# Row maxima in single PSUM banks of one ring of six, part of v's split on GpSimd, and a written-out order for the first two pairs of heads

## The chip, the cores and the metric

The kernel runs on one core of one Trainium2 chip. The metric is device time in microseconds (us), the median of repeated runs. A core has five instruction queues that matter here: TensorE (PE, matmuls; PEld is its weight load), VectorE (DVE), ScalarE (ACT), GpSimd (POOL) and SyncE (SP, which only issues DMAs). Each runs its instructions in order and stops at the first one whose inputs, or whose output buffer, aren't ready.

## What is computed

Attention in which a query sees only the keys of its own cluster, and behind it a mixture of experts on the attention's output:

```python
def _attn_ref(q, k, v, centroids):
    ...
    q_assign = np.argmax(np.einsum('bhsd,hcd->bhsc', q_n, c_n), axis=-1)
    k_assign = np.argmax(np.einsum('bhsd,hcd->bhsc', k_n, c_n), axis=-1)
    mask = q_assign[:, :, :, None] == k_assign[:, :, None, :]
    scores = scale * np.matmul(q, k.transpose(0, 1, 3, 2))
    scores = np.where(mask, scores, -1000000000.0)
    scores = scores - np.max(scores, axis=-1, keepdims=True)
    attn = np.exp(scores)
    ...
    return np.matmul(attn, v)
```

Four batches, eight heads, 768 tokens, 64 columns a head, 16 clusters. The experts (8 of them, the best two for each of the 3072 tokens) take 512 columns to 1024 and back.

## The kernel before

The heads go in 16 pairs (four batches of four pairs); a pair is `p`, its two heads `s`. Float32 numbers are split into an upper and a lower half, so that TensorE can work with shorter types and lose little. For each pair:

- `load_qk` brings q and k, `a_hi` (ACT) and `a_lo` (DVE, some on POOL) split them. From pair 2 on `a_hi` writes a copy into a PSUM bank and `a_lo` subtracts from it. `b_place` copies the halves by DMA into the two big operand tiles A and Bt (three sets, used in turn).
- `a_sims`, `a_copy`, `a_turn`, `a_max1`, `a_ge`, `a_ky`, `a_max2`, `a_eq`, `a_mask` find the clusters; `b_mask` adds them to A by DMA, so that one matmul gives a score with the mask in it.
- `b_max` (line 541): for each head and each of six blocks of 128 queries, two matmuls of 128x384 (L546) give all 768 scores of upper halves; one DVE reduction over 768 columns (L549) takes their maximum. The two matmuls write a tile `wide` of two PSUM banks, of which there is one.
- `b_neg` and `b_negT` turn the 12 maxima of a pair into two rows of Bt.
- `scores` (L577): per step four matmuls and two exponentials (ACT, L578); `split_p` (L589, POOL) takes the lower half of 768 exponentials; `values` (L610 to L616) multiplies with v, four steps later.

v comes in half batches of four heads: `load_v`, `v_max` (DVE, L386), `v_scale` (a matmul, L397, and two small DVE operations) and, head by head, `v_split` (L411): ACT scales v into a PSUM bank (L415), ACT takes the upper half of it (L416), DVE subtracts for the lower half (L417).

PSUM has eight banks. In the attention one is `aux` (maxima and small sums), one `av` (the values), two are `wide`, and four are a `ring` that everything else takes its banks from (`ps()`). In the experts `wide`'s two banks are given to the ring as `ring2`.

The order of the work is written by hand. `attention` fills a table `sched`: `at(step, f, ...)` puts a part at a step, with steps of 12 to a pair; numbers for it stand in `AT` (lines 28 to 40). Each step then issues its table entries around `scores`, `split_p` and `values` of a step four back. Everything at step -24 comes first, before the first scores (step 0); the first pair's parts stand there (`f0`), head by head, the second pair has numbers of its own (`p1`, steps -21 to -13, and its masks at 0.333). An order in the table is the order in every engine's queue. A ring bank is handed out when its part is issued, and the first instruction that writes it waits until the last reader of the tile that had the bank is done.

Of the kernel before, what the change touches and what calls it, by code (L numbers as in the profile page):

```python
# [9 lines left out]
F32 = mybir.dt.float32  # L10
# [26 lines left out]
    thr=5.0, bmax0=[-20.333, -1.333], bstep0=[1.0, 0.667], neg0=[-15.0, 2.667], negT0=[-14.667, 3.333],  # L37
    p1=dict(hstep=0, hi=[-21.0, -21.0], lo=[-13.667, -13.667], place=-13.0, sims=-18.333, copy=-18.333, turn=-16.333, max1=-14.333,
            ge=-14.333, max2=-14.333, eq=-14.333, ky=-14.333, mask=0.333, bmask=0.333),
# [7 lines left out]
class Kernel:  # L47
    def __init__(self, ctx, tc, qk, v, cent, w_gate, w_noise, noise, w1, w2, out):
# [16 lines left out]
        self.more_banks, self.turns = None, 0  # L65
# [131 lines left out]
    def attention(self, ctx):  # L197
        nc, tc = self.nc, self.tc
        B, H, S, D, NJ = self.B, self.H, self.S, self.D, self.NJ
        self.psum2 = ctx.enter_context(tc.tile_pool(name="psum2", bufs=1, space=PSUM))  # L200
# [25 lines left out]
        for p in range(NP):  # L226
            b, hp = divmod(p, H // 2)
            w = 12 * (p - 2)
            if hp == 0:
                for g in range(2):  # L230
                    v = w + 24 * g
                    V = T["fv"][g] if p == 0 else T
                    at(22.333 if (b, g) == (1, 0) else v + V["v"], self.load_v, b, g)
# [17 lines left out]
            if p == 0:  # L251
                f0 = lambda f, *a: at(-24, f, *a)
                f0(self.load_qk, 0, 0)
                f0(self.load_qk, 0, 1)
                f0(self.load_qk, 1)
                for s in range(2):
                    for i in range(2):
                        f0(self.a_hi, p, i, s)
                    if s == 0:
                        f0(self.c_turn)  # L260
                        f0(self.fixed_init, 0)
                        f0(self.constants2)
                    for i in range(2):
                        f0(self.a_lo, p, i, s)
                f0(self.fixed_init, 1)
                f0(self.fixed_init, 2)
                f0(self.b_place, p, 0, 0)
                for s in range(2):
                    for f in (self.a_sims, self.a_copy, self.a_turn, self.a_max1, self.a_ge, self.a_ky, self.a_max2,
                              self.a_eq, self.a_mask, self.b_mask):  # L270
                        f0(f, p, s)
                    f0(self.b_place, p, 1, s)
                    if s == 0:
                        f0(self.b_place, p, 0, 1)
# [1137 lines left out]
```

## Time and profile before

| | us |
|---|---|
| median of 3 runs | 1099.83 (1098.12 to 1108.2) |
| the profiled execution | 1095.88 |
| its span, first to last instruction | 1094.0 |
| TensorE busy | 968.3 (89%) |
| VectorE busy | 662.2 (61%) |
| GpSimd busy | 549.9 (50%) |
| ScalarE busy | 493.0 (45%) |

The span has two parts: the attention, to about 518 us, and the experts behind it. The shares are means over both. A matmul's busy time holds its pipeline, so TensorE that reads as busy is not at its peak. The granted TensorE clock is a share of 2.4 GHz: 1.00 is 2.4, 0.50 is 1.2.

### The profile page before, as it was taken

Reading aid. Unit: us, or ns where it says so; the run is one execution under the profiler, and the core shown is the slowest. Engines: PE = TensorE matmul, PEld = TensorE weight load, DVE = VectorE, ACT = ScalarE, POOL = GpSimd, SP = SyncE. Lnnn points to the kernel's source line nnn. Section 1 sums busy time; section 2 is a strip of 40 time slices with the busy share of each in tenths; the row PEclk is TensorE's granted clock in tenths of the full one; section 3 lists DMA queues with packets and bytes.
Section 4 is the critical chain, followed back from the end, with each engine's and each line's share of the span. In section 5 each row is a group of like instructions: output and inputs, shape, how many; then the busy total and the mean of one; then the engine's idle time right before and its main releaser. Section 6 shows DMA issues by size and latency. Waiting matters only on the chain.

```text
span 1094.0 us, 21139 instructions
## 1 busy us (share of the span) xinstructions
PE 968.3 (89%) x8020; PEld 615.8 (56%) x8020; DVE 662.2 (61%) x1254; ACT 493.0 (45%) x1100; POOL 549.9 (50%) x609
## 2 busy tenths in 40 slices
PE   4378788888888888879999999999999999999994
PEld 1256667666677667668455545545455454554542
DVE  4456677787777877778655654555445564454511
ACT  3245665665667575647713522415224152241510
POOL 9135566666996679777244524325242252433211
PEclk9868999999999999999999999999999999999998
DMA  5636487776878787633639772946829266293200
GB/s 157 175 88 168 117 195 188 165 190 150 192 168 181 158 182 170 139 120 86 175 105 212 172 204 81 209 133 161 199 86 239 95 168 194 74 202 122 63 33 33
DMA packets 164252, 162.74 MB, mean 149 GB/s; under 512 B 87945, under 2 KB 140041, under 8 KB 164146
## 3 DMA queue, kind: packets, MB, share of 16 engines
q1 hardware_dynamic: 150476, 124.65, 48.6%
q0 software_dynamic: 13296, 36.38, 11.7%
q8 instruction: 64, 1.05, 0.4%
q10 hardware_dynamic: 374, 0.32, 0.1%
q14 instruction: 42, 0.34, 0.1%
HBM read 78.21 MB, written 26.51 MB: 96 GB/s over the span
## 4 chain that ended last, share of the span: by engine, by line
PE 44%; issue 5%; POOL 1%; ACT 0%; DVE 0%; DMA 0%; POOLq 0%; ACTq 0%
PE ring L1301 22%; PE ring L1339 20%; PE ring L1329 1%; POOL out L1351 1%; POOL xt L1314 1%; PE ring L1332 1%; PE ring L1206 0%; PE ring L721 0%; PE ring L886 0%; DMA out<-yo,idx 0%; PE ring L729 0%; PE ring L1197 0%; ACT gxT L723 0%; ACT w2t L1185 0%; DVE pl L589 0%
## 5 line engine op out<-in xcount | busy, mean ns | idle before, releaser
L589 POOL TENSOR_TENSOR pl<-pe 128x768 f16<-128x768 f32 x173 | 253.5, 1472 | 144.7 <-ACT pe L578 93.5
L1301 PE MATMUL ring<-xT,w1t 128*128 128x416 f16 (+2 forms) x1536 | 272.8, 339 | 0.1
L1339 PE MATMUL ring<-w2t,hT 128*128 128x512 f16 x1152 | 252.5, 379 | 0.6 <-ACT w2t L1185 0.5
L578 ACT ACTIVATE pe<-ring 128x384 f32<-128x384 f32 x384 | 168.2, 489 | 171.0 <-PE ring L577 165.2
L549 DVE TENSOR_REDUCE aux<-wide 128x1 f32<-128x768 f32 x192 | 185.0, 964 | 89.3 <-PE wide L546 86.5
L1301 PEld LDWEIGHTS <-w1t 128*128 128x128 f16 x1536 | 149.3, 98 | 118.8 <-issue 0.8
L546 PE MATMUL wide<-A 128*128 128x384 f32 x384 | 126.7, 409 | 71.1 <-DVE aux L549 60.0
L1178 ACT ACTIVATE hr<-ring 128x416 f32<-128x416 f32 (+2 forms) x128 | 66.5, 519 | 270.7 <-PE ring L1301 268.3
L1339 PEld LDWEIGHTS <-hT 128*128 128x128 f16 x1152 | 112.2, 98 | 134.1 <-issue 1.5
L1351 POOL DMA_INDIRECT out<-yo,idx x52 | 62.4, 1199 | 226.9 <-DVE yo L1347 109.8
L577 PE MATMUL ring<-A 128*128 128x384 f32 x384 | 138.2, 360 | 3.6 <-ACT pe L578 1.9
L577 PE MATMUL ring<-B 128*128 128x384 f32 x384 | 132.7, 346 | 0.0
L1181 DVE TENSOR_TENSOR hT<-hr,hT 128x416 f16<-128x416 f32 (+3 forms) x128 | 71.2, 559 | 83.8 <-ACT hT L1180 83.5
L546 PEld LDWEIGHTS wide<-A 128*128 128x128 f32 x384 | 62.8, 203 | 96.9 <-DVE aux L549 81.7
L1347 DVE SCALAR_TENSOR_TENSOR yo<-ring,we,xt 128x512 f32<-128x512 f32 (+1 forms) x49 | 36.7, 748 | 122.8 <-PE ring L1339 107.5
L610 PE MATMUL av<-vv,pe 128*128 128x65 f16 x1152 | 98.9, 196 | 0.1
L612 PE MATMUL av<-vv,pe 128*128 128x64 f16 x1152 | 97.6, 193 | 0.0
L1281 POOL DMA_INDIRECT xg<-xs,idx x52 | 56.4, 1085 | 81.6 <-DMA xT<-xg 71.3
L610 PEld LDWEIGHTS <-pe 128*128 128x128 bf16 x1152 | 78.4, 99 | 27.0 <-issue 25.4
L612 PEld LDWEIGHTS <-pe 128*128 128x128 bf16 x1152 | 79.2, 99 | 0.2
L577 PEld LDWEIGHTS ring<-A 128*128 128x128 f32 x384 | 74.5, 194 | 8.4 <-ACT pe L578 3.7
L577 PEld LDWEIGHTS ring<-B 128*128 128x128 f32 x384 | 74.7, 194 | 0.0
(218 smaller groups left out, 1177.3 us busy)
## 6 DMA issues: line engine op xcount, KB each, us to landing
stg<-in_moe_w SPq DMA_DIRECT2D x64, 512.0 KB
qt<-in_qk SPq DMA_DIRECT2D x15, 768.0 KB
A<-hl SPq DMA_DIRECT2D x28, 384.0 KB
B<-hl SPq DMA_DIRECT2D x28, 384.0 KB
B<-hl SPq DMA_DIRECT2D x32, 192.0 KB
vt<-in_v SPq DMA_DIRECT2D x8, 768.0 KB
out<-zt SPq DMA_DIRECT2D x12, 512.0 KB
xs<-xh SPq DMA_DIRECT2D x15, 384.0 KB
```

The source lines that it names most:

```text
L546: nc.tensor.matmul(t[:, n], A[:, 0, s, j * 128:j * 128 + 128], A[:, 1, s, n * 384:n * 384 + 384], start=True, stop=True)
L549: nc.vector.tensor_reduce(self.aux[:, c:c + 1], t, axis=XY, op=OP.max, negate=True)
L577: nc.tensor.matmul(t, M[:, 1 - qi, s, ks], M[:, qi, s, ns], start=not qi, stop=bool(qi))
L578: nc.scalar.activation(pe[:, n], t, AF.Exp, scale=self.scale)
L589: (nc.vector if last else nc.gpsimd).tensor_tensor(lo, pe, hi, op=OP.subtract)
L610: nc.tensor.matmul(av[:, j, :], ph[:, js], vv[:, hh, kj, 64:129], start=(kc == 0 and j == 0), stop=False, skip_group_check=True)
L612: nc.tensor.matmul(av[:, j, :64], ph[:, js], vv[:, hh, kj, 0:64], start=False, stop=False, skip_group_check=True)
L1178: nc.scalar.activation(r[:, :n], p, AF.Relu, scale=2.0 ** -HT)
L1181: nc.vector.tensor_tensor(h1, r[:, a:b], h0, op=OP.subtract)
L1301: nc.tensor.matmul(p, self.w1t[:, wi, c, f * 128:f * 128 + 128], self.xT[e][:, c, xi, n0:n1], start=(i == 0), stop=(i == 3 * ND - 1))
L1339: nc.tensor.matmul(p, self.hT[:, hi, f, t * 128:t * 128 + 128], self.w2t[:, wi, f], start=(i == 0), stop=(i == 3 * NF - 1))
L1351: i = nc.gpsimd.indirect_dma_start(out=self.out, out_offset=bass.IndirectOffsetOnAxis(ap=en[:r], axis=0), in_=yo[:r], in_offset=None, boun ...
```

## The change

Four things are done.

1. The ring has six banks from the start, `wide` and `ring2` are gone. `b_max` takes two single banks of the ring, and each gets a reduction of its own over 384 columns: the first into `aux` as before, the second into a small SBUF tile `mm`. `b_neg` has one more operation, the minimum of both (the maxima are negated).
2. `v_split` scales v in place in SBUF, and GpSimd subtracts.
3. The first pair's parts, the second pair's up to its masks, and the first `load_v` are issued in one written-out order (`first`). The numbers `p1`, `bmax0[0]`, `neg0[0]`, `negT0[0]` are gone.
4. The lower halves of the first pair's second head go from POOL to DVE, those of the second pair from DVE to POOL. Four placements of the first pair (`b_place(0, 1, 0, dma)`) are issued by ACT's queue.

```diff
     def ps(self):
-        self.turns += 1
-        if self.more_banks and self.turns % 3 == 0:
-            return self.more_banks.tile([128, 512], F32, name="ring2", bufs=2)
-        return self.psum.tile([128, 512], F32, name="ring", bufs=4)
+        return self.psum.tile([128, 512], F32, name="ring", bufs=6)
...
-                f0(self.load_qk, 0, 0)
...
+    def first(self, do):
+        dma = self.nc.scalar
+        do(self.load_qk, 0, 0)
+        do(self.load_qk, 0, 1)
+        do(self.load_qk, 1)
...
+        do(self.b_place, 0, 1, 0, dma)
+        do(self.a_copy, 1)
+        do(self.b_place, 0, 1, 1)
+        do(self.load_v, 0, 0)
+        for j in range(self.NJ):
+            do(self.b_max, 0, 0, j)
+            if j == 1:
+                do(self.a_turn, 1)
+        for i in range(2):
+            do(self.b_place, 1, i)
+        do(self.b_neg, 0, 0, 1)
+        do(self.b_negT, 0, 0, 1)
+        for f in (self.a_max1, self.a_ge, self.a_ky, self.a_max2, self.a_eq, self.a_mask, self.b_mask):
+            do(f, 1)
...
     def v_split(self, b, g, h):
         nc, D = self.nc, self.D
         vv, am = self.vv[b, g], self.am[b, g]
-        t = self.ps()[:, :384].rearrange("p (j d) -> p j d", d=D)
-        nc.scalar.activation(t, self.vt[b, g][:, h], AF.Copy, scale=am[:, 2:3])
+        t = self.vt[b, g][:, h]
+        nc.scalar.activation(t, t, AF.Copy, scale=am[:, 2:3])
         nc.scalar.activation(vv[:, h, :, 64:128], t, AF.Copy)
-        nc.vector.tensor_tensor(vv[:, h, :, 0:64], t, vv[:, h, :, 64:128], op=OP.subtract)
+        nc.gpsimd.tensor_tensor(vv[:, h, :, 0:64], t, vv[:, h, :, 64:128], op=OP.subtract)
...
-            (self.nc.gpsimd if s else self.nc.vector).tensor_tensor(hl[:, 3 - 3 * i, a:b], qt[:, i, a:b], hl[:, 1 + i, a:b],
+            (self.nc.gpsimd if p else self.nc.vector).tensor_tensor(hl[:, 3 - 3 * i, a:b], qt[:, i, a:b], hl[:, 1 + i, a:b],
...
     def b_max(self, p, s, j):
 
         nc, st, A = self.nc, self.st[p], self.A[p % 3]
+        if (s, j) == (0, 0):
+            st["mm"] = self.wk.tile([128, 2 * self.NJ], F32, name="mm")
         c = self.NJ * s + j
-        t = self.psum2.tile([128, 2, 512], F32, name="wide", bufs=1)[:, :, :384]
         for n in range(2):
-            nc.tensor.matmul(t[:, n], A[:, 0, s, j * 128:j * 128 + 128],
+            t = self.ps()[:, :384]
+            nc.tensor.matmul(t, A[:, 0, s, j * 128:j * 128 + 128],
                              A[:, 1, s, n * 384:n * 384 + 384], start=True, stop=True)
-        c += 488 + 12 * (p % 2)
-        nc.vector.tensor_reduce(self.aux[:, c:c + 1], t, axis=XY, op=OP.max, negate=True)
+            m = 488 + 12 * (p % 2) + c
+            o = st["mm"][:, c:c + 1] if n else self.aux[:, m:m + 1]
+            nc.vector.tensor_reduce(o, t, axis=X, op=OP.max, negate=True)
 
     def b_neg(self, p, s, n):
 
-        v, W, c = self.nc.vector, n * self.NJ, 488 + 12 * (p % 2) + self.NJ * s
-        o = self.aux[:, c:c + W]
+        v, W, c = self.nc.vector, n * self.NJ, self.NJ * s
+        m = 488 + 12 * (p % 2) + c
+        o = self.aux[:, m:m + W]
         hi, lo = (self.nm[:, W * i:W * i + W] for i in range(2))
+        v.tensor_tensor(o, o, self.st[p]["mm"][:, c:c + W], op=OP.min)
```

What this does to SP's queue at the start, before the first scores. `A_115` and `B_118` (after: `A_112` and `B_115`) are the second pair's A and Bt, `qt` is a load of q and k (the first in these rows belongs to the third pair, the second to the fourth), `vt` the first load of v. Before:

```order
L373 DMA qt<-in_qk 128x1536
L516 DMA A_115<-xt 64x4x384
L516 DMA A_115<-xt 32x2x384 x2
...
L516 DMA B_118<-xt 32x4x384
L380 DMA vt<-in_v 128x1536
L373 DMA qt<-in_qk 128x1536
L516 DMA A_115<-mk 16x2x384 x2
```

After:

```order
L403 DMA vt<-in_v 128x1536
L539 DMA A_112<-xt 64x4x384
L539 DMA A_112<-xt 32x2x384 x2
...
L539 DMA B_115<-xt 32x4x384
L539 DMA A_112<-mk 16x2x384 x2
L396 DMA qt<-in_qk 128x1536 x2
```

The load of v went ahead of the second pair's ten placements; the load of the third pair's q and k went from ahead of them to behind them and behind the mask's two.

What it does to DVE's queue in the middle of the attention, where a half batch of v is split. Line 549 (after: 575) is the maximum, 439 (462) the lower halves of q and k, 417 the lower half of v. Before:

```order
L549 TENSOR_REDUCE aux<-wide 128x1
L439 TENSOR_TENSOR hl<-ring,hl 128x384
L417 TENSOR_TENSOR vv<-ring,vv 128x6x64
L549 TENSOR_REDUCE aux<-wide 128x1
L417 TENSOR_TENSOR vv<-ring,vv 128x6x64
L549 TENSOR_REDUCE aux<-wide 128x1
```

After:

```order
L575 TENSOR_REDUCE aux<-ring 128x1
L575 TENSOR_REDUCE mm<-ring 128x1
L462 TENSOR_TENSOR hl<-ring,hl 128x384
L575 TENSOR_REDUCE aux<-ring 128x1
L575 TENSOR_REDUCE mm<-ring 128x1
```

Each maximum has become two rows, and the subtractions of v that stood between the maxima are gone from this queue.

Those subtractions stand in POOL's queue now, between the lower halves of the exponentials (line 617, before 589), which followed each other there before. After:

```order
L617 TENSOR_TENSOR pl<-pe 128x768
L440 TENSOR_TENSOR vv<-vt,vv 128x6x64
L617 TENSOR_TENSOR pl<-pe 128x768
L440 TENSOR_TENSOR vv<-vt,vv 128x6x64
L617 TENSOR_TENSOR pl<-pe 128x768 x2
L709 TENSOR_TENSOR xh<-xp,xh 128x6x64
```

Each is an operation of 128 partitions by 384 elements on the queue that had none of them.

## Rows read from the trace of the kernel before

**Rows 1.** Busy us by stage: PE, PEld, DVE, ACT, POOL; clock, DMA share, GB/s.
```profile
40.00:130.00 90.00, 63.07 (x579) 47.98 (x577) 51.65 (x91) 45.18 (x101) 37.03 (x30) 0.83 0.52 128
130.00:477.50 347.50, 291.01 (x3798) 241.86 (x3796) 259.31 (x537) 219.61 (x515) 256.52 (x226) 1.00 0.77 176
518.30:1094.00 575.70, 559.62 (x3001) 284.15 (x2996) 294.72 (x514) 192.08 (x411) 197.85 (x278) 0.99 0.55 141
```

**Rows 2.** Waits from 130 to 477.5: us in total, times, longest.
```profile
DVE aux L549 <- PE wide L546: 58.3, 81, 2.1
PEld wide L546 <- DVE aux L549: 45.8, 44, 2.0
PE wide L546 <- DVE aux L549: 35.2, 41, 1.7
...
DVE vv L417 <- ACT vv L416: 18.9, 22, 1.4
```

**Rows 3.** PE's waits from 40 to 130: the same columns.
```profile
PE wide L546 <- DVE aux L549: 13.0, 16, 1.9
PE ring L397 <- DVE vm L386: 9.2, 1, 9.2
```

**Rows 4.** Timeline at 60: start, us, engine, line, idle before and what ended it.
```profile
59.97 0.16 DVE L558 SCALAR_TENSOR_TENSOR nm<-aux,nm 128x6 fp32r<-128x6 f32 x1
...
61.26 0.62 PE L546 MATMUL wide<-A 128*128 128x384 f32 x2 [0.60 <-DVE aux L549]
...
61.92 0.97 DVE L549 TENSOR_REDUCE aux<-wide 128x1 f32<-128x768 f32 x1 [0.26 <-PE wide L546]
62.94 0.62 PE L546 MATMUL wide<-A 128*128 128x384 f32 x2 [1.06 <-DVE aux L549]
```

**Rows 5.** Groups by line: count, busy us, mean ns of one, idle before.
```profile
L589 POOL TENSOR_TENSOR pl<-pe 128x768 f16<-128x768 f32 x173 | 253.5, 1472 | 144.7 <-ACT pe L578 93.5 <-PE av L616 32.6 <-ACT nt L565 10.7
...
L681 POOL TENSOR_TENSOR xh<-xp,xh 128x384 f16<-128x384 f32 x26 | 24.0, 924 | 16.7 <-ACT xh L677 16.7
...
L417 DVE TENSOR_TENSOR vv<-ring,vv 128x384 f16<-128x384 f32 x32 | 17.8, 557 | 26.8 <-ACT vv L416 26.8
```

**Rows 6.** Three DVE reductions by line: ns shortest/median/longest, first and last start, forms.
```profile
L549 DVE TENSOR_REDUCE aux<-wide x192: 954/967/967, 18.6 to 494.3; 128x1 f32<-128x768 f32 x192
...
L475 DVE TENSOR_REDUCE mx<-ring x17: 358/547/549, 9.1 to 452.1; 128x24 f32<-128x384 f32 x15, 128x12 f32<-128x192 f32 x2
...
L386 DVE TENSOR_REDUCE vm<-vt x8: 1743/1745/1756, 50.7 to 416.0; 128x1 bf16<-128x1536 f32 x8
```

**Rows 7.** Timeline of the start (SPq is SP issuing DMAs).
```profile
11.06 1.95 POOL L441 TENSOR_TENSOR hl<-qt,hl 128x384 fp32r<-128x384 f32 x2
...
16.56 4.10 SPq L516 DMA_DIRECT2D A<-hl  x6
...
20.23 0.73 POOL L363 MEMSET B<- 2x768 f32 x1
...
25.32 0.53 SPq L373 DMA_DIRECT2D qt<-in_qk  x1
...
40.04 1.13 ACT L578 ACTIVATE pe<-ring 128x384 f32<-128x384 f32 x2 [4.89 <-PE ring L577]
...
46.29 0.33 SPq L380 DMA_DIRECT2D vt<-in_v  x1
...
50.71 1.76 DVE L386 TENSOR_REDUCE vm<-vt 128x1 bf16<-128x1536 f32 x1 [9.89 <-DMA vt<-in_v]
```

**Rows 8.** Pairs 4, 7, 8 and 14, columns as in rows 1.
```profile
187.30:215.30 28.00, 24.00 (x313) 19.84 (x311) 19.75 (x41) 18.27 (x43) 19.29 (x16) 1.00 0.76 167
...
275.00:302.60 27.60, 23.32 (x308) 19.70 (x306) 20.51 (x35) 18.00 (x41) 26.40 (x28) 1.00 0.82 193
302.60:330.60 28.00, 23.96 (x313) 19.83 (x311) 19.73 (x41) 18.28 (x43) 25.49 (x26) 1.00 0.76 163
...
477.50:500.30 22.80, 19.66 (x283) 17.52 (x281) 19.78 (x38) 10.72 (x27) 19.15 (x26) 1.00 0.08 27
```

More of the change, by code (lines that the diff above doesn't have):

```diff
@@ L36 @@
         {'v': 9.0, 'vscale': 11.667, 'am': 13.333, 'amstep': 0.333, 'vsplit': 15.0, 'vstep': 1.667}],
[L37 to L39 removed]
+    thr=5.0, bmax0=-1.333, bstep0=0.667, neg0=2.667, negT0=3.333,
     bm={1: (14.667, 0.5, 20.333, 22.0), 2: (13.333, 0.75, 21.667, 22.333)})
@@ L265, in attention @@
[L265 to L274, printed above, removed]
@@ L275, in attention @@
-                for s in range(2):
-                    for j in range(NJ):
-                        at(T["bmax0"][s] + T["bstep0"][s] * j, self.b_max, p, s, j)
-                    at(T["neg0"][s], self.b_neg, p, s, 1)
-                    at(T["negT0"][s], self.b_negT, p, s, 1)
-            else:
-                P = T["p1"] if p == 1 else T
-                w = 0 if p == 1 else w
-                for i in range(2):
-                    for s in range(2) if p > 1 else [None]:
-                        at(w + P["hi"][i] + (s or 0) * P["hstep"], self.a_hi, p, i, s)
-                        at(w + P["lo"][i] + (s or 0) * P["hstep"], self.a_lo, p, i, s)
-                for i in range(2):
-                    at(w + P["place"], self.b_place, p, i)
-                for k, f in (("sims", self.a_sims), ("copy", self.a_copy), ("turn", self.a_turn), ("max1", self.a_max1),
-                             ("ge", self.a_ge), ("ky", self.a_ky), ("max2", self.a_max2),
-                             ("eq", self.a_eq), ("mask", self.a_mask), ("bmask", self.b_mask)):
-                    at(w + P[k], f, p)
+                self.first(lambda f, *a: at(-24, f, *a))
@@ new lines, in attention @@
+                for j in range(NJ):
+                    at(T["bmax0"] + T["bstep0"] * j, self.b_max, p, 1, j)
+                at(T["neg0"], self.b_neg, p, 1, 1)
+                at(T["negT0"], self.b_negT, p, 1, 1)
+            else:
+                if p > 1:
+                    for i in range(2):
+                        for s in range(2):
+                            at(w + T["hi"][i] + s * T["hstep"], self.a_hi, p, i, s)
+                            at(w + T["lo"][i] + s * T["hstep"], self.a_lo, p, i, s)
+                        at(w + T["place"], self.b_place, p, i)
+                    for k, f in (("sims", self.a_sims), ("copy", self.a_copy), ("turn", self.a_turn), ("max1", self.a_max1),
+                                 ("ge", self.a_ge), ("ky", self.a_ky), ("max2", self.a_max2),
+                                 ("eq", self.a_eq), ("mask", self.a_mask), ("bmask", self.b_mask)):
+                        at(w + T[k], f, p)
```

63 lines of the change are left out of this document (42 added, 21 removed).

## The prediction

> **What bounds the kernel now.** I read the busy times by stage first. From 518 us on TensorE is busy for 559.62 of 575.70 us [rows 1]: nothing in the change touches the experts but the ring, which has six banks there before and after, so this stage keeps its length and only starts earlier or later. What counts is the attention. From 130 to 477.5 us, where twelve pairs (2 to 13) run at 28.96 us each on average, no engine is full: PE 291, DVE 259, POOL 257, ACT 220 of 347.5 us, the DMA engines 77% [rows 1]. So engines wait for each other, and the waits say how. PE waits 35.2 us for the maxima's reduction, in 41 of the 144 maxima of this stage, its weight loads 45.8 us, and DVE in turn waits 58.3 us for the maxima's matmuls [rows 2]. Of PE's 56.5 us without work this is the largest piece by far. The timeline shows the loop: matmuls at 61.26, reduction at 61.92, the next matmuls at 62.94 [rows 4]. There is one `wide`, so a maximum takes 1.68 us from start to start even with nothing else on DVE, and whenever DVE has other work in front, PE stands, with the scores and values queued behind. One such piece of other work is v's lower half: DVE stands 18.9 us at L417 for ACT [rows 2], with the next maximum's reduction behind it.
>
> From 40 to 130 us two pairs need 90 us. Here PE waits 13.0 us for reductions and once 9.2 us at the small matmul of `v_scale` [rows 3]. The latter is a late load: v was issued at 46.29, behind the second pair's placements, and `v_max` began at 50.71, after 9.89 us of standing [rows 7].
>
> **The change part by part.** I work against the profiled execution's own 1095.88 us (span 1094.0 and 1.88 around it); the median shown is 3.95 us above it, so I put the difference on the median.
>
> *Single banks, DVE's price.* A reduction over 768 columns takes 0.967, one over 384 columns of a ring bank 0.547 (the L475 form with 24 results), over 1536 columns 1.745 [rows 6]. Two of 0.547 cost 0.127 more than one of 0.967; the straight line through 768 and 1536 (1.013 ns a column, 0.189 us fixed) gives 0.578 for 384, thus 0.189 more. These are the bounds; I take 0.127, since that row reads the same memory and as many columns. 144 maxima make 18.3 us (27.2 at the upper bound), and the minimum in `b_neg`, a small operation like L558 with 0.16 us [rows 4], about 2 us more in twelve pairs. Against it 24 subtractions of 0.557 [rows 5], 13.4 us, leave DVE, and the 18.9 us of standing before them. DVE's work becomes 259.3 + 18.3 + 2 - 13.4 = 266 us of 347.5: more, but with room.
>
> *Single banks, PE's gain.* A maximum no longer waits for the one before as such, but for whoever had its bank last. I counted the hand-overs in the banks of the built program for pairs 2 to 13 apart from the last: of 272 banks that maxima take, 101 were left by a maximum one step before, 35 two steps before, 99 by an exponential of the same or the last step, the rest by small things. Before, it was the maximum before in 136 of 136. So the tie to the last reduction is gone in 63% of the banks, and where it stays, the first of the two reductions frees its bank early. With the standing at L417 gone as well, I take two thirds of the 35.2 us as won, 23.5. The least is nothing (the waits move to the hand-overs from ACT and from the last maximum), the most 45.8, all that the weight loads wait, because PE counts as busy while its pipeline drains.
>
> *POOL's price.* 24 subtractions of 384 elements in this stage at 0.924 each (L681 has the same shape and types) [rows 5] are 22.2 us: POOL 256.5 + 22.2 = 279 of 347.5. Spread evenly this hides behind POOL's waits for the exponentials. It isn't spread evenly: in pairs 7 and 8, where the lists are written by indirect DMAs, POOL is busy 26.40 of 27.60 and 25.49 of 28.00 us, in pair 4 only 19.29 of 28.00 [rows 8]. Pairs 11 and 12 repeat this. With two subtractions each, pair 7 needs 28.2 and pair 8 27.3 us of POOL, so these four pairs can hardly be shorter than they are, apart from the lag that five buffers of lower halves allow. A third of 23.5 us belongs to them, 7.8; I strike half of that, 4. Gain of the stage: 19.5 us.
>
> Moving work from DVE to POOL has a second side: whether the two hinder each other. The reductions take between 954 and 967 ns in all 192 cases [rows 6], though POOL is busy three quarters of the time, so POOL's reads slow none of these. The Trainium skill ("Perfetto Trace Analysis", Optimizing Scalar/DVE Operations) warns that GpSimd and DVE share an SBUF read port, so that moving work between those two might not help. By that rule each subtraction on POOL would hold a DVE instruction for its own length: 24 x 0.924 = 22 us, which would leave nothing of the stage's gain. The trace doesn't bear this out for reductions, whose input is in PSUM.
>
> *The start.* v's load is issued before the second pair's placements, right behind the first pair's, which ended at 20.66 (16.56 + 4.10) for its second head [rows 7]. 4.4 us from issue to use (46.29 to 50.71) puts v ready near 25 to 30, well ahead, so the 9.2 us at `v_scale` go. What is late next: the third pair's q and k. Their load was issued at 25.32 [rows 7] and now stands behind ten placements and two mask DMAs, and ACT's queue has their split ahead of the first exponential, in the old order and the new. I estimate its time from rows: POOL's clearing of the second set ended at 20.96 with 1.95 us of the first pair's halves before it, which it no longer does, so 19.0; two subtractions of 768 elements at 1.47 to 1.95 end by 22.5; ten placements at 0.68 each (six took 4.10) by 29.3; the masks wait for the second pair's clusters, near 33; the load is issued at 34 and usable 4.4 later, at 38.4; two ACT operations of 0.5 and the first exponential begins near 39.5, where it was at 40.04 [rows 7]. So this costs nothing by itself, and nothing is won before the first exponential either; if the DMAs are slower than this, each us is lost. Bounds: -1 to +8; I take 0.
>
> Behind that, the 31 maxima from 40 to 130 wait 13.0 us; two thirds go, 8.7. A reduction here also has DVE mostly idle (51.65 of 90 us) [rows 1], so its price is hidden.
>
> **Sum.** -9.2 (v's load), -8.7 (early maxima), -19.5 (later maxima): -37.4 us. 1095.88 becomes 1058.5, the median 1099.83 becomes 1062.4. I forecast 1062 us. A measurement of this kernel can tell about 1% from no change, that is 11 us.
>
> **The rivals.**
>
> *More comes free.* Without `wide`, the engines run into each other as loosely as in pair 14, which has eight maxima left and where DVE is busy 19.78 of 22.80 us, 87% [rows 8]. The fullest engine of the stage is then POOL with 279 us; at 88% that is 317 instead of 347.5, -30. Early, all 13.0 and 9.2 us go, and PE, denser, is granted 1.00 instead of 0.83 [rows 1] for some of the 90 us, worth perhaps 5. Together -57: 1043. For it speaks that no engine is above 84% anywhere but in the list pairs; against it that everything is queued in a fixed order and 101 banks keep the tie.
>
> *POOL takes over, or the ring's hand-overs do.* POOL's four full pairs don't shrink, and there and elsewhere the maxima now wait for ACT's exponential of the same step (72 of the 272). The stage wins 5, the early one 4, v's load 9.2: -18, 1082. The shared read port, if it hindered DVE, would end at the same place.
>
> *The change does little.* The third pair's load comes 8 us later than I worked out, which eats v's gain, and the reductions' standing only changes its owner: 1097.
>
> *Slower.* DVE becomes the pace. Its place is every maximum: PE and DVE keep their waits for each other (DVE stands 58.3 us for the matmuls [rows 2], though the bank is another), and the price is each reduction's longer work. If DVE's idle time of 88 us in the stage stays, 266 + 88 = 354 us, and with the upper bound of 0.189 it is 363, +16; early +6 for 31 maxima; v's load -9: +13, 1113. It decides from the point where DVE's idle time in this stage falls by less than about 10 us. Against it: 18.9 of that idle time is L417's and goes with it.
>
> **How the numbers follow.** I give the forecast 0.44, more free 0.22, POOL or the hand-overs 0.18, little 0.09, slower 0.07. The first three are all below 1088.8, 1% under the median: faster 0.84; within 1% 0.09; slower by over 1% 0.07. The range reaches from the larger gain with its bound (45.8 instead of 30 in the stage: 1033) to past the third case, 1090; outside are the last two and a little below.
>
> **What would show it.** Right: `v_max` begins before 43 us and PE has no long wait at `v_scale`; PE's waits for the maxima's reductions from the first exponential to pair 13 are under 16 us instead of 48.2; a reduction over 384 columns takes 0.54 to 0.58 us; twelve pairs average near 27.3 us, pairs 7, 8, 11 and 12 stay near 27 to 28 with POOL over 95% busy; the experts' stage is 575 us as before. Wrong: the first exponential later than 42; waits of PE for ACT's exponentials or DVE of a similar sum in the place of the old; pairs that stay at 29; reductions of over 0.6 us.

## The result, and the profile after

The changed kernel takes 1058.26 us (median of 4 runs, 1056.35 to 1059.37) against 1101.19 us of the kernel before in the same session (4 runs, 1098.12 to 1108.2). The ratio is 0.96 with a 95% interval of 0.9551 to 0.9649: 4.0% faster. The forecast was 1062 us, 3.4% under its median. The profiled execution took 1059.37 us with a span of 1057.5, 36.5 us shorter than before; the sum had said 37.4. By the medians the gain is 42.9 us: the four executions of before lie 10 us apart, and the profiled one is 5.3 us under their median.

Where the 36.5 us went can be read from when each pair's first exponential starts (24 exponentials belong to a pair). The first one of all comes at 46.2 us instead of 40.0, which is 6.2 lost. Pairs 0 and 1 take 67.1 us instead of 89.9 (-22.8), pairs 2 to 13 take 329.2 instead of 347.5 (-18.3), pairs 14 and 15, up to where the row of the experts begins, 0.5 us behind the last exponential, take 39.3 instead of 40.9 (-1.6).

The busy times by stage, of after, with the columns of [rows 1]: pairs 0 and 1, pairs 2 to 13, the experts. Between the second and the third row stand pairs 7 and 8, which answer to [rows 8].

```profile
46.20:113.30 67.10, 54.71 (x568) 42.99 (x568) 49.10 (x116) 44.32 (x100) 43.54 (x38) 0.91 0.54 129
113.30:442.50 329.20, 297.12 (x3798) 243.78 (x3796) 254.52 (x669) 220.20 (x514) 275.21 (x250) 0.98 0.83 184
...
252.20:278.40 26.20, 23.07 (x291) 18.79 (x290) 20.11 (x45) 17.89 (x42) 25.05 (x28) 1.00 0.89 200
278.40:305.40 27.00, 24.24 (x316) 19.72 (x316) 19.35 (x52) 18.21 (x44) 25.86 (x29) 1.00 0.89 177
...
481.90:1057.50 575.60, 559.53 (x2998) 284.05 (x2994) 294.83 (x514) 192.07 (x411) 197.92 (x278) 0.99 0.57 142
```

The experts take 575.6 us, as before. In pairs 2 to 13 PE is without work for 32.1 of 329.2 us, where it was 56.5 of 347.5. So PE's waiting fell by 24.4 us and its own busy time grew by 6.1 (291.01 to 297.12). POOL does 18.7 us more there, DVE 4.8 us less. In pairs 0 and 1 PE is without work for 12.4 us instead of 26.9, and its own work there takes 8.4 us less (63.07 to 54.71) at a granted clock of 0.91 instead of 0.83.

The waits of after: from 113 to 442.5 (first PE's two largest, then DVE's largest from 113.3 on), with the columns of [rows 2].

```profile
PE ring L531 <- DVE oh L522: 6.5, 8, 1.5
PE ring L605 <- ACT pe L606: 4.3, 8, 0.7
...
DVE aux L575 <- PE ring L571: 54.6, 61, 2.8
```

In [rows 2] PE stood 35.2 us and its weight loads 45.8 us for a maximum's reduction. Neither row has a successor: no maximum's matmul (L571) is listed as waiting for a reduction into `aux`, all that PE still waits for the reductions (L575) is 1.4 us at a small matmul of the lists (L837), and the largest wait that is left is 6.5 us for the clusters' comparison. DVE still waits 54.6 us for the maxima's matmuls (58.3 before), but PE no longer waits for these reductions in turn.

PE's waits in pairs 0 and 1, which answer to [rows 3]:

```profile
PE ring L605 <- ACT pe L606: 13.2, 3, 11.2
PE ring L571 <- DVE hl L462: 5.3, 2, 5.0
...
PE ring L420 <- DVE vm L409: 0.2, 1, 0.2
```

The 9.2 us at `v_scale` are 0.2 (L420), the 13.0 us for reductions are gone. Of the first new row 11.2 us lie around the first exponential. The 5.0 us of the second are another event, at 70.2 us, which ring and v without the new order show as well. The timeline shows the first (columns as in [rows 4]; the last three rows are a maximum in the middle of the attention):

```profile
16.20 0.57 DVE L575 TENSOR_REDUCE aux<-ring 128x1 f32<-128x384 f32 x1 [2.62 <-PE ring L571]
16.68 0.55 DVE L575 TENSOR_REDUCE mm<-ring 128x1 f32<-128x384 f32 x1
...
22.69 1.05 SPq L403 DMA_DIRECT2D vt<-in_v  x1
23.79 8.21 SPq L539 DMA_DIRECT2D A<-xt  x6
33.45 4.20 SPq L539 DMA_DIRECT2D B<-xt  x4
37.75 2.35 SPq L539 DMA_DIRECT2D A<-mk  x2
40.20 1.00 SPq L396 DMA_DIRECT2D qt<-in_qk  x2
...
45.31 0.49 ACT L453 ACTIVATE ring<-qt 128x384 f32<-128x384 f32 x1 [9.93 <-DMA qt<-in_qk]
45.83 0.49 ACT L454 ACTIVATE hl<-ring 128x384 fp32r<-128x384 f32 x1
46.22 0.87 ACT L606 ACTIVATE pe<-ring 128x384 f32<-128x384 f32 x2
46.36 0.56 DVE L462 TENSOR_TENSOR hl<-ring,hl 128x384 fp32r<-128x384 f32 x1 [11.34 <-ACT hl L454]
46.83 1.75 DVE L409 TENSOR_REDUCE vm<-vt 128x1 bf16<-128x1536 f32 x1
...
262.11 0.59 PE L571 MATMUL ring<-A 128*128 128x384 f32 x2
262.57 0.57 DVE L575 TENSOR_REDUCE aux<-ring 128x1 f32<-128x384 f32 x1 [0.81 <-PE ring L571]
263.04 0.55 DVE L575 TENSOR_REDUCE mm<-ring 128x1 f32<-128x384 f32 x1
```

The third pair's q and k are requested at 40.20, and ACT, whose queue holds their split ahead of the first exponential, stands until 45.31. DVE stands with it, 11.34 us, with `v_max` queued behind. So v, which was there in time, is still not touched before 46.83. The first scores are ready in the meantime and wait.

Reductions and subtractions by line: ns shortest, median and longest, first and last start, forms, as in [rows 6].

```profile
L575 DVE TENSOR_REDUCE aux<-ring x192: 543/566/567, 16.2 to 457.6; 128x1 f32<-128x384 f32 x192
L575 DVE TENSOR_REDUCE mm<-ring x192: 535/547/558, 16.7 to 458.0; 128x1 f32<-128x384 f32 x192
...
L440 POOL TENSOR_TENSOR vv<-vt,vv x32: 872/893/917, 53.8 to 423.3; 128x384 f16<-128x384 f32 x32
```

### The profile page after: what moved, and what is told of

The parts are those of the page before. It is cut to its first block, busy times and chain, and to the rows that moved or that the text cites. A ratio compares the mean times of both kernels' runs of the same rounds, so it can differ in the third digit from the quotient of the medians.

```text
span 1057.5 us, 21351 instructions
## 1 busy us (share of the span) xinstructions
PE 965.5 (91%) x8020; PEld 613.8 (58%) x8020; DVE 655.0 (62%) x1431; ACT 493.5 (47%) x1100; POOL 577.9 (55%) x641
## 4 chain that ended last, share of the span: by engine, by line
PE 46%; issue 5%; POOL 2%; ACT 0%; DVE 0%; DMA 0%; POOLq 0%; ACTq 0%
PE ring L1328 22%; PE ring L1366 21%; PE ring L1356 1%; POOL xt L1341 1%; POOL out L1378 1%; PE ring L1359 1%; PE ring L1233 0%; DMA out<-yo,idx 0%; PE ring L749 0%; PE ring L914 0%; PE ring L757 0%; PE ring L1224 0%; ACT gxT L751 0%; ACT w2t L1212 0%; DVE pl L617 0%
## 5 line engine op out<-in xcount | busy, mean ns | idle before, releaser
L605 PE MATMUL ring<-A 128*128 128x384 f32 x384 | 141.6, 369 | 20.1 <-ACT pe L606 17.5
L575 DVE TENSOR_REDUCE aux<-ring 128x1 f32<-128x384 f32 x192 | 107.9, 562 | 77.2 <-PE ring L571 72.9
L571 PE MATMUL ring<-A 128*128 128x384 f32 x384 | 124.0, 395 | 21.6 <-DVE hl L462 6.5
L575 DVE TENSOR_REDUCE mm<-ring 128x1 f32<-128x384 f32 x192 | 105.0, 547 | 0.2
L638 PEld LDWEIGHTS <-pe 128*128 128x128 bf16 x1152 | 79.0, 99 | 27.3 <-issue 24.9
L605 PEld LDWEIGHTS ring<-A 128*128 128x128 f32 x384 | 74.0, 193 | 32.8 <-ACT pe L606 27.1
L571 PEld LDWEIGHTS ring<-A 128*128 128x128 f32 x384 | 65.4, 200 | 36.4 <-ACT pe L606 12.2
```

What stands on the lines that cost most here:

```text
L571: nc.tensor.matmul(t, A[:, 0, s, j * 128:j * 128 + 128], A[:, 1, s, n * 384:n * 384 + 384], start=True, stop=True)
L575: nc.vector.tensor_reduce(o, t, axis=X, op=OP.max, negate=True)
L605: nc.tensor.matmul(t, M[:, 1 - qi, s, ks], M[:, qi, s, ns], start=not qi, stop=bool(qi))
L638: nc.tensor.matmul(av[:, j, :], ph[:, js], vv[:, hh, kj, 64:129], start=(kc == 0 and j == 0), stop=False, skip_group_check=True)
```

## The experiments

The runs were made in three groups, each on another chip, and the chips differ: the kernel before took 1116.55 us (13 runs; the first four experiments below), 1116.94 (7; the next four) and 1098.54 (7; the last four). So each kernel is given as a ratio to before on its own chip, and times are compared only inside a group. Even ratios don't carry over exactly: the early third load, run on two of the chips, gave 0.9451 and 0.9529, with separate intervals. Where two groups have to be compared, the stages of the profiles are used. `ring`, `v` and `order` stand for the change's parts 1, 2, and 3 with 4. The theory was that the one `wide` tile was the tie and that most of the gain is the ring's. The rivals were that the gain came from v's subtractions leaving DVE, from the order at the start, or that POOL or the ring's hand-overs had become the limit.

| kernel | median us | ratio, 95% interval | first exp. | pairs 0-1 | pairs 2-13 | pairs 14-15 |
|---|---|---|---|---|---|---|
| before | 1101.19 | 1 | 40.0 | 89.9 | 347.5 | 40.9 |
| after | 1058.26 | 0.96, 0.9551 to 0.9649 | 46.2 | 67.1 | 329.2 | 39.3 |
| ring only | 1067.49 | 0.9576, 0.9538 to 0.9615 | 32.9 | 80.6 | 330.7 | 42.5 |
| v only | 1102.57 | 0.9875, 0.984 to 0.991 | 40.0 | 82.3 | 346.0 | 53.0 |
| order only | 1112.65 | 0.9965, 0.9943 to 0.9988 | 46.7 | 77.7 | 352.9 | 51.9 |
| after, third load early | 1055.36 | 0.9451, 0.9417 to 0.9485 | 36.6 | 68.1 | 326.4 | 45.1 |
| after, again | 1064.97 | 0.9546, 0.9511 to 0.9582 | 46.2 | 67.0 | 325.8 | 44.5 |
| ring, order | 1070.35 | 0.9584, 0.9556 to 0.9612 | 46.2 | 67.8 | 329.3 | 47.3 |
| ring, v | 1066.96 | 0.9559, 0.953 to 0.9588 | 32.6 | 79.7 | 327.2 | 44.0 |
| two own banks | 1086.79 | 0.9733, 0.9707 to 0.9758 | 46.1 | 70.5 | 337.6 | 52.1 |
| ring, v, v's load early | 1054.52 | 0.9601, 0.9564 to 0.9638 | 34.5 | 73.7 | 328.4 | 39.4 |
| after, third load early, again | 1047.26 | 0.9529, 0.9497 to 0.956 | 36.4 | 67.4 | 326.6 | 39.3 |
| half the later reductions doubled | 1085.24 | 0.9886, 0.9854 to 0.9918 | 45.4 | 69.0 | 346.5 | 42.8 |
| five banks | 1066.38 | 0.9705, 0.9676 to 0.9735 | 46.6 | 71.8 | 334.2 | 39.3 |

### One part alone: ring, v, order

Each is the kernel before with one part taken over from the diff shown above. The ring alone:

```diff
-        t = self.psum2.tile([128, 2, 512], F32, name="wide", bufs=1)[:, :, :384]
...
+            t = self.ps()[:, :384]
...
+            nc.vector.tensor_reduce(o, t, axis=X, op=OP.max, negate=True)
```

> The kernel before with the ring of six and the maxima in single banks alone; v's lower halves stay on DVE, the start keeps its old order. Theory 1 (the single wide tile was the tie): PE's waits for the maxima's reductions fall from 60 us to under 20, pairs 2 to 13 take about 333 us instead of 347, the early pairs win about 9: 1076 to 1082 us. Theory 2 (DVE was held by v's split and the tie was only where it showed): the waits stay above 40 us and the time is within 6 us of before, since two reductions cost DVE more than one.

v's split alone (scaled in place in SBUF, subtracted on GpSimd):

```diff
-        nc.vector.tensor_tensor(vv[:, h, :, 0:64], t, vv[:, h, :, 64:128], op=OP.subtract)
+        nc.gpsimd.tensor_tensor(vv[:, h, :, 0:64], t, vv[:, h, :, 64:128], op=OP.subtract)
```

> The kernel before with v's lower halves on GpSimd alone. Theory 1: DVE's 26.8 us of standing at the split go, but the one wide tile still ties each maximum to the last: 3 to 7 us faster, 1093 to 1098 us. Theory 2: 15 us faster or more, 1085 us or less. A third theory, GpSimd as the pace in the list pairs (7, 8, 11, 12): no change or slower there, those four pairs at 28 us and over.

The order alone (`first`, the halves' engines and ACT's placements, with `wide` kept):

```diff
+        do(self.load_v, 0, 0)
+        for j in range(self.NJ):
+            do(self.b_max, 0, 0, j)
```

> The kernel before with the written-out start alone. Theory 1 (the late load of the third pair's q and k, 6 us, takes back most of what v's early load gives, 9 us): first exponential near 46 us instead of 40, the wait at v's scale gone, 2 to 6 us faster in all, 1094 to 1098 us. Rival (the early load of v counts in full): 9 us faster or more, 1091 us or less. Rival (the start's lateness carries through): slower by 5 us.

Measured: 0.9576, 0.9875 and 0.9965. The ring alone reaches what the whole change reaches (0.96 and 0.9546 in two sessions); the other two, alone, bring 1.3% and 0.4%. For the ring, theory 1 had the mechanism and too small a gain (1076 to 1082 us would be a ratio of 0.98): it left out what happens ahead of the first exponential. For the order, theory 1's 2 to 6 us held (3.9). For v it missed: 14 us where it had said 3 to 7, close to theory 2's 15. The stages don't show v as the cause of that: pairs 0 and 1 are 7.6 us shorter than in the profile of before, but PE's waits there are the old ones (12.3 us for reductions, 9.3 at `v_scale`), and 5.3 of the 7.6 are PE's own work (57.74 us instead of 63.07) at a granted clock of 0.98 instead of 0.83. Where the rest of the 14 us comes from stays open.

PE's largest wait for a reduction from 113 to 440 us, with v only (first row) and with the order only (second):

```profile
PE wide L546 <- DVE aux L549: 31.4, 31, 2.0
```

```profile
PE wide L574 <- DVE aux L577: 35.9, 40, 1.9
```

It is the 35.2 of [rows 2], hardly less, and pairs 2 to 13 keep 346.0 and 352.9 us. With the ring only, no such row is left, and these pairs take 330.7 us. So in the middle the tie was `wide`, not what stood between the reductions on DVE. Rows of the ring-only run say more: the stage (first fence), and its start (second), where the first head's six maxima begin; the third fence has the first and the last of the same six maxima in before.

```profile
113.50:444.20 330.70, 298.36 (x3798) 242.42 (x3796) 265.60 (x693) 219.57 (x515) 256.07 (x226) 0.99 0.82 184
```

```profile
18.12 0.57 DVE L547 TENSOR_REDUCE aux<-ring 128x1 f32<-128x384 f32 x1 [1.07 <-PE ring L543]
18.60 0.55 DVE L547 TENSOR_REDUCE mm<-ring 128x1 f32<-128x384 f32 x1
19.07 0.56 DVE L547 TENSOR_REDUCE aux<-ring 128x1 f32<-128x384 f32 x1
...
25.13 0.54 SPq L368 DMA_DIRECT2D qt<-in_qk  x1
...
31.14 0.49 ACT L425 ACTIVATE ring<-qt 128x384 f32<-128x384 f32 x1 [2.37 <-DMA qt<-in_qk]
```

```profile
18.55 0.97 DVE L549 TENSOR_REDUCE aux<-wide 128x1 f32<-128x768 f32 x1 [1.34 <-PE wide L546]
...
29.20 0.97 DVE L549 TENSOR_REDUCE aux<-wide 128x1 f32<-128x768 f32 x1 [1.10 <-PE wide L546]
```

First, the starts of reductions in a row are 0.465 us apart though each lasts 0.55 to 0.57, here as in after: DVE begins the next while the last one ends. DVE's busy time in the stage is 265.6 us, 6.3 more than before, where I had reckoned 20.3. Second, the ring wins time before the first exponential, by itself: the six maxima of the first head take 6.6 us (18.12 to 24.67) where they took 11.6 (18.55 to 30.17), and the first exponential comes at 32.9 us, 7.1 earlier.

### The third pair's load

The loss at the first exponential should be the late load. Its request goes ahead of v's and the second pair's placements; all else is as in after.

```diff
-            if p > 1:
+            if p > 2:
                 at(w + T["qk"], self.load_qk, p)
...
         do(self.b_place, 0, 1, 1)
+        do(self.load_qk, 2)
         do(self.load_v, 0, 0)
```

> The changed kernel with the third pair's q and k loaded right before the first v, ahead of the second pair's placements. Theory 1: ACT waited 9.9 us for that load alone; the first exponential comes near 40 us instead of 46.2 and the time falls by about 6 us, to 1052. Rival (the start is bound by the bytes of the placements, or the wait is handed on to the second pair's maxima, whose placements now come later): first exponential earlier, but the second pair's maxima wait and the time is within 2 us of the changed kernel's 1058.

Measured: 0.9451, its interval below that of after again (0.9511 to 0.9582, on another chip with nearly the same time for before). The first exponential comes at 36.6, 3.4 us earlier than theory 1 had it, and pairs 0 and 1 are 1 us longer: the rival, in which the wait is only handed on, is out. The same kernel was run once more on the chip where before takes 1098.54 us:

> The changed kernel with the third pair's q and k loaded ahead of the second pair's placements, again, beside the others of this call: 8 to 10 us faster than the changed kernel's ratio of 0.9546, about 0.945, with the first exponential near 37 us. If the old order with an early v does as well, the rest of the written-out order is worth nothing; if it is slower by 4 us or more, it is worth that.

Measured: 1047.26 us (1044.92 to 1047.86), 0.9529. The forecast ratio of 0.945 was missed, since it came from the other chip; against after's 0.96 it is 7.8 us, just under the 8 to 10 expected, and the two intervals overlap by a little. The first exponential came where it was expected. It is the version with the shortest profile, 1045.4 us of span against after's 1057.5. Its queues at the start:

```profile
23.00 0.69 SPq L397 DMA_DIRECT2D qt<-in_qk  x1
23.73 0.48 SPq L404 DMA_DIRECT2D vt<-in_v  x1
24.26 11.68 SPq L540 DMA_DIRECT2D A<-xt  x6
...
35.52 0.49 ACT L454 ACTIVATE ring<-qt 128x384 f32<-128x384 f32 x1
36.05 0.49 ACT L455 ACTIVATE hl<-ring 128x384 fp32r<-128x384 f32 x1
36.44 0.87 ACT L607 ACTIVATE pe<-ring 128x384 f32<-128x384 f32 x2
```

The split no longer waits for the load, and the first exponential is at 36.4 instead of 46.2, 9.8 us earlier. Pairs 0 and 1 take 67.4 us as in after, so nothing of it is paid back. One request was moved and all else kept, so its place behind ten placements and two masks is what held the first exponential from 36.4 to 46.2. `v_max` now begins at 37.05: v had been there in time.

### The parts on top of the ring

After once more, unaltered, for comparison on this group's chip:

> The changed kernel unaltered, beside the next three on one chip, since the kernel before took 1116 us on the chip of the first four runs and 1101 on that of the result. If the parts add, its ratio lies at or below the ring's alone (0.958), about 0.955 to 0.962; the late load of the third pair's q and k shows again as a first exponential at 45 to 47 us.

Ring and order, with v's split as in before (two operations of ACT through a ring bank, subtraction by DVE):

> The changed kernel with v's lower halves back on DVE (and v scaled into a ring bank). Theory 1 (with the ring the maxima no longer wait for DVE, so what else stands in DVE's queue hardly matters): within 4 us of the changed kernel, pairs 2 to 13 within 4 us of its 329. Theory 2 (the split on GpSimd carries a part of the gain of its own): 8 us or more slower than the changed kernel. Theory 3 (GpSimd is the pace in the list pairs): faster than the changed kernel by 2 us or more, in pairs 7 to 9 and 11 to 13.

Ring and v, with the order of before:

> The changed kernel with the old order at the start (ring of six and v's split on GpSimd, no written-out order). Theory 1 (the new order's early v gains about what its late third load loses): first exponential between 32 and 36 us, pairs 0 and 1 about 80 us instead of 67, the time within 5 us of the changed kernel. Rival (the new order is worth its 9 us for v's load): 8 us slower than the changed kernel.

Measured: 0.9546, 0.9584 and 0.9559. v's split on GpSimd brings 5.4 us on top of the ring (1070.35 - 1064.97), with intervals that overlap; that is between the theories, 1.4 us over what theory 1 allowed and short of theory 2. The order brings 2 us, which isn't told apart from nothing and is what theory 1 of its run had said. The stages say why. With ring and v the first exponential comes at 32.6 us and pairs 0 and 1 take 79.7; with the order added it comes at 46.2 and they take 67.0. The sums are 112.3 and 113.2: the order moved v ahead and the third pair's load back, and the two cancel.

Pairs 2 to 13 of after again (first fence) and of ring with order (second):

```profile
113.20:439.00 325.80, 293.38 (x3798) 241.03 (x3797) 254.30 (x670) 219.88 (x514) 275.50 (x250) 0.99 0.85 187
```

```profile
114.00:443.30 329.30, 298.36 (x3798) 241.69 (x3796) 265.23 (x694) 219.10 (x515) 255.76 (x226) 0.99 0.83 184
```

24 subtractions take 10.9 us off DVE and put 19.7 on POOL, and the stage is 3.5 us shorter. So theory 3, GpSimd as the pace in the list pairs, finds no support: pairs 7 to 9 take 26.2, 26.3 and 27.1 us with the subtractions on POOL, and 26.4, 26.3 and 27.6 without. Pairs 7 and 8 say little by themselves, because POOL is full in both kernels (25.0 and 25.2 us with, 24.9 and 25.1 without): with three subtractions in pair 7 it does ten lower halves of the exponentials there instead of twelve, and makes up for it in pair 9. Pair 9 says more: POOL is busy 26.8 of 27.1 us with the subtractions and 21.0 of 27.6 without, and the pair is no longer for it. And pair 4, where POOL has room (19.4 of 26.4 us), is no shorter than the list pairs.

### Only v's load early, in the old order

Ring and v with before's order, in which only the first load of v goes ahead of the second pair's placements, and the third pair's load keeps its early place:

```diff
-                    at(22.333 if (b, g) == (1, 0) else v + V["v"], self.load_v, b, g)
+                    if b or g:
+                        at(22.333 if (b, g) == (1, 0) else v + V["v"], self.load_v, b, g)
...
+                f0(self.load_v, 0, 0)
```

> The ring of six, v's split on GpSimd and the old order at the start, with one thing of the new order: the first v is loaded ahead of the second pair's placements (and of the third pair's q and k, which stay ahead of the placements). Theory (of the written-out order, v's early load is the part that pays, and the third pair's late load the part that costs): first exponential at 33 to 37 us, pairs 0 and 1 about 70 us instead of 80, 8 to 10 us faster than ring and split with the old order (ratio near 0.947). Rival (the rest of the new order is needed for it): within 3 us of that kernel, ratio near 0.956.

Measured: 0.9601. As a ratio this looks like the rival's 0.956, but that came from another chip, so the stages decide. The first exponential is at 34.5 and pairs 0 and 1 take 73.7 us, together 108.2; ring and v without the early load have 112.3, after has 113.3, the early third load 103.8. By these profiles this one line is worth 4 us, not the 8 to 10 of the theory, and its start is 5 us shorter than that of after's written-out order; the rest of that order is worth another 4 us at the start once its own late load is put right. By the medians on the same chip it is 7.3 us (1054.52 and 1047.26), with separate intervals. 0.9601 itself doesn't differ from after's 0.96, which was measured in another session, so the 5 us over after rest on the profiles alone. Why v's early load pays only half: with it, PE stands once for 10.6 us in these pairs, at 51.84, for a placement (`A<-hl`), where ring and v without it stood 11.6 us at `v_scale`; the early third load has no wait there over 3.4. What in the rest of the order (the halves' engines, the placements on ACT's queue, the sequence) does this was not tried piece by piece.

### How many banks, and whose

Two single banks of their own for the maxima, and four for the ring:

```diff
-        return self.psum.tile([128, 512], F32, name="ring", bufs=6)
+        return self.psum.tile([128, 512], F32, name="ring", bufs=4)
...
-            t = self.ps()[:, :384]
+            t = self.psum.tile([128, 512], F32, name="wide", bufs=2)[:, :384]
```

> The changed kernel, but the maxima take their single banks from two banks of their own, and the ring has four as before. If what counts is that a maximum may start before the last one's reduction is through (banks freed one by one), it keeps most of the gain: within 6 us of the changed kernel. If what counts is the choice among six banks, each maximum is still tied to the reduction of the one before, PE's waits for reductions come back to 20 us or more in pairs 2 to 13, and it is 12 to 25 us slower than the changed kernel.

One common ring, but of five banks:

```diff
-        return self.psum.tile([128, 512], F32, name="ring", bufs=6)
+        return self.psum.tile([128, 512], F32, name="ring", bufs=5)
```

> The changed kernel with a ring of five banks instead of six. If the number of banks sets the gain, it lies between the changed kernel (0.9546) and the one with two banks of their own for the maxima (0.9733): 6 to 14 us slower than the changed kernel, with PE's waits for reductions or exponentials up by as much. If five already loosen the tie, it is within 4 us.

Measured: 0.9733 and 0.9705. The waits of PE and its weight loads from 113 to 440 us, with two own banks (first) and with five common ones (second):

```profile
PE wide L571 <- DVE aux L575: 17.9, 23, 1.4
PEld wide L571 <- DVE aux L575: 25.7, 26, 1.7
```

```profile
PE ring L571 <- ACT pe L606: 6.4, 23, 0.3
PEld ring L571 <- ACT pe L606: 19.7, 50, 0.6
```

With own banks the tie to the last reduction is about half as strong as in [rows 2], 17.9 instead of 35.2 us, and pairs 2 to 13 take 337.6 us, about halfway (347.5 before, 325.8 for after on the same chip). So splitting the tile is about half of the stage's gain; the other half comes with the choice among six banks. The whole is 21.8 us slower than after on its chip, as the second theory said (its waits of 20 us or more are 17.9), but 7.6 of that lies in pairs 14 and 15 (see the last section). With five, the maxima wait more for the exponentials, in short pieces (PE 6.4 us instead of 1.1, its weight loads 19.7 instead of 9.7 in after), and the stage takes 334.2 us, 7.6 more than the early third load on the same chip; against after's 0.96 the time is 11.5 us longer, inside the 6 to 14 of the first theory. By the stages, five common banks do no worse than six that are split into two and four (334.2 and 337.6); by the ratios, whose intervals overlap and which come from two chips, they can't be told apart.

### Is DVE the pace?

Every second maximum's later reduction is done twice (96 of 192, not the 79 of the expectation):

```diff
+            if n and j % 2:
+                nc.vector.tensor_reduce(o, t, axis=X, op=OP.max, negate=True)
```

> The changed kernel with a price added on DVE and nothing else: the reduction of the second bank is done twice in every second maximum, 6 x 0.547 = 3.3 us of DVE more in each pair, 79 of 192 places doubled at half (52 us in all). DVE in pairs 2 to 13 goes from 21.2 to 24.5 of 27.2 us. Theory (with the ring DVE has room, its added work hides): pairs 2 to 13 grow by less than a third of the 39 us added there, 12 us or less. Rival (DVE is the pace now): they grow by most of it, 27 us or more.

Measured: 0.9886, about 31 us more than after at 0.96, for 96 x 0.557 = 53 us of added work. The stage, in a window of 350 us:

```profile
113.00:463.00 350.00, 304.47 (x3855) 246.21 (x3852) 296.03 (x748) 222.90 (x518) 278.34 (x252) 0.99 0.80 178
```

Pairs 2 to 13 grow by 17.3 us against after (329.2 to 346.5), by 19.9 against the early third load on the same chip (326.6), for 72 x 0.557 = 40 us of work: 43% to 50%. That lies between the theories. DVE has some room, not much: on the way from 255 of 329 us busy to 296 of 350 each further us cost nearly half a us. So the slower rival's mechanism exists once DVE is given this much more work; that the change itself pays none of it isn't shown.

## Why the prediction was right, and which steps were not

**The late maxima** (-19.5): measured -18.3, and -21.7 against [rows 1] in the second run of after. The wait of 35.2 us was the right row, and `wide` its cause, as the ring-only run shows. It went whole, not by two thirds, but PE's waiting in all fell by 24.4 us, near the 23.5 of the term: about 11 us came back as other waits. Within the term, the 4 us that I struck for the list pairs were wrong: I had them stay at 27 to 28 us because POOL would be full, and reckoned 28.2 us of POOL for pair 7. POOL is full, but with less work than that (25.05 of 26.20 and 25.86 of 27.00 us, since it puts lower halves off), and pairs 7, 8, 11 and 12 took 26.2, 27.0, 25.2 and 27.1 us. Without POOL's added work they are hardly different (26.4, 26.3, 26.4 and 26.3). That the term still came out near its 19.5 is luck: PE's own busy time grew by 6.1 us. Most of that lies in pair 6, 32.9 us in this profile and 30.3 in the second run of after: the granted clock was 0.50 from 230 to 240 us there.

**The load of the third pair** (0, bounds -1 to +8): this is the step that failed, by +6.2 us, inside its bound. The prediction said "the load is issued at 34 and usable 4.4 later, at 38.4". It was issued at 40.20 and usable at 45.31. POOL's halves ended at 22.68 as reckoned (22.5); the time of the placements was mis-sized. "0.68 each (six took 4.10)" came from the first pair's placements, but here six took 8.21 us, and ten with their gap 13.86 (23.79 to 37.65) instead of 6.8. The trace of before had the row of these very placements, the second pair's:

```profile
25.95 12.45 SPq L516 DMA_DIRECT2D A<-xt  x6
38.51 3.86 SPq L516 DMA_DIRECT2D B<-xt  x4
```

Of the 12.45 us SP stood 7.8 for DVE's lower half, which the change moves to POOL. Taking that off would have left 4.7, so the step was not careless; what it left out is that SP stands for other things as well. In after the ten requests themselves took 9.3 us, single ones up to 1.63 instead of 0.68, and SP stood 2.8 us ahead of the sixth and 1.4 ahead of the first of Bt; the trace puts both down to the landing of earlier DMAs (`A<-xt`, `B<-nt`). What lies behind these landings and the long requests isn't settled. The masks then went out at 37.75, not 33. I also missed that the ring speeds up the start: in the old order it brings the first exponential to 32.9. Of the 13 us between that and 46.2 the late load is 9.8, as the experiment with the early load shows; the other 3.5 belong to the rest of the new order.

**v's early load and the early maxima** (-9.2 and -8.7, together -17.9): from the first exponential on, pairs 0 and 1 won 22.8 us; counted with its delay, 16.6. Of the 22.8, waits are 14.5, less than the 17.9 of the two terms; the other 8.4 are PE's own work at a higher granted clock, which the prediction had only in its rival of more gain ("worth perhaps 5"). So the start came out near its sum because the late load and the clock nearly cancel, which is luck too. v's early load as the only change of the order was worth 4 us, not 9.2: the wait moves to a placement. The wait at `v_scale` went, as said. "`v_max` begins before 43 us" didn't hold: it began at 46.83, not for want of v but because DVE's queue had the third pair's lower half in front. The same late load did both: with that load early it begins at 37.05.

**DVE's price** (18.3 and 2 us): 6.3. The duration of 0.547 for 384 columns was right (0.535 to 0.567). The step from durations to engine time was not: in a row they start 0.465 us apart. The Trainium skill says as much ("Perfetto Trace Analysis", Optimizing Scalar/DVE Operations): part of a DVE instruction's profiled time overlaps with the next one. I took it for hidden anyway, so the sum didn't suffer, but the slower rival was priced 14 us too dear (18.3 and 2 instead of 6.3).

**v on POOL.** 0.893 us each (I used 0.924), hidden. The Trainium skill, in the same section, also warns that work moved between DVE and GpSimd might not help because of a shared SBUF read port. Here that doesn't show: the reductions, whose input is in PSUM, keep 0.547 and 0.566 us, and the stage is 3.5 us shorter with the subtractions on GpSimd than without.

**The rivals.** More free (1043) needed the early stage without the late load; the version with the early load, at 0.9529, would be 1048 on the median shown. POOL or the hand-overs (1082): no run shows POOL as the pace, and the hand-overs begin to cost with one bank fewer. The experts' 575 us held. Two statements don't come out of their rows: the lower end of the range, 1033, should be 1027 (1043 less 15.8), and "no engine is above 84% anywhere but in the list pairs" overlooks PE in pair 4, 24.00 of 28.00 us [rows 8]. Neither bears on the result.

## What to carry to other kernels

A buffer of which there is one ties its producer to its consumer however much room both engines have: look for a wait of many short pieces between the same two lines, and try giving the tile its buffers from a common ring; a private pair brought only half here. When a load is moved ahead in an in-order queue, work out what now goes out last, and look on every engine's queue for what stands behind that one's first use; here that took back all that the new order had won in pairs 0 and 1. When you price a row of DMA requests, look for the same requests in the old trace and take their standing apart from their issuing. Price instructions that run in a row by the distance of their starts, not by their durations.

## What was not expected of the hardware

The chips differ by 1.7% for the same program (1098.54 and 1116.94 us). On the two slower ones all eight profiles have waits that the trace puts down to something outside the core (`remote`), 4.8 to 10.1 us of them on ACT in the experts; none of the other six profiles has any. In the three kernels there that keep separate banks for the maxima, another one, of DVE, stands in pair 14 (the largest in the others there is 5.0 us, of ACT, with ring and order). With two own banks:

```profile
DVE aux L575 <- remote: 8.1, 1, 8.1
```

With v only and with the order only it is 10.8 and 10.0 us, and pairs 14 and 15 take 52 to 53 us, where the kernels with the common ring take 42 to 47 on these chips. No profile of the kernel before was taken there, so whether this is why the change gains more on those chips (0.9546 instead of 0.96, with intervals that overlap; for the early third load 0.9451 instead of 0.9529, with separate ones) stays open; no run was made for it. The granted clock fell to 0.50, which is 1.2 GHz, for 10 us in pair 6 of after, though PE was busy for 89% of the stretch around it. Just before it fell, from 226 to 230, PE was busy for only 2.50 of 4.00 us, with 10 matmuls after 53 in the 4 us ahead, and stood for ACT's exponentials; the second run of after has no such fall in this pair. No run tried its cause. The window of after around that pair, with the columns of [rows 1]:

```profile
219.00:253.00 34.00, 30.32 (x351) 25.11 (x350) 25.11 (x76) 19.85 (x46) 19.79 (x19) 0.85 0.70 151
```

The clock's column reads 0.85 there, where the whole stage has 0.98.
